# Weight chunks of the first expert layer: both words of the fp32 split kept in DRAM and loaded again, instead of one fp32 word that is split anew

## The chip, the cores and the metric

The kernel runs on one core of a Trainium2 chip. The metric is the device time of one execution in microseconds (us); lower is better. The core has five engines with a queue of instructions each: TensorE (PE: matmuls, and PEld, its weight loads), VectorE (DVE), ScalarE (ACT), GpSimd (POOL) and SyncE (SP), which here only issues DMAs. An engine takes its instructions in the order of its queue; semaphores tie the queues together.

## The reference, cut to what matters

```
x = attention(q, k, v)                                  # 4 x 8 heads, 576 tokens, keys and values pooled by 8
x: 2304 tokens x 512
x = (sigmoid(x @ w_gate) * (x @ w_val)) @ w_out         # "first layer": 512 -> 1536 -> 512
P = 8 rounds of row and column normalisation of exp(x @ gate)
out = sum over 8 experts of P[:, e] * (relu(x @ w1[e]) @ w2[e])
```

The three matrices of the first layer come in as float64. Every matmul of the layers is done on two fp32r words of each operand, the high word `hi` (the operand rounded) and the low word `lo` (the operand less `hi`), in three passes: hi.hi, hi.lo, lo.hi.

## The kernel before

The 2304 tokens are six blocks of 384. For each block j the first layer runs over twelve slices f of the hidden width. A pair (j, f) is a step, and there are 72. A step takes three weight chunks of 128 x 512, named g (gate), v (value) and o (out): 12 matmuls with g into a bank `pg`, 12 with v into `pv`, then sigmoid on ACT, the product with `pv` on DVE (line 821), the split of the product into `h` (ACT line 822, DVE line 825), and, one step later, 12 matmuls with o into four banks `big` (`x2_step`, line 560). The attention of the next block is cut into stages that are laid between these matmuls: scores (line 351), maximum and subtraction (369, 370), one exponential for the block (ACT line 393), sums (DVE 397), division (407), turning (PE 422, copied by ACT 424), product with the values (437), split into `xs` (ACT 447, DVE 448). The order of everything is the order in which the program writes it. The function `slot` decides how much narrowing and attention work goes between two matmul groups, by a running estimate `until` of when PE and DVE will be done.

**Narrowing.** Each of the 36 chunks (12 slices, three kinds) is read once as float64 (`load_wide`, four buffers `wide`) and made into fp32 `made` (four buffers) by `narrow_tick`: one scaling on ACT (185) and five operations on DVE (165, 166, 169, 175, 179; for the first twelve chunks 179 is on POOL). The steps of blocks 0, 1 and 2 are interleaved by slice, two slices at a time: `steps1` runs (0,0) to (0,3), (1,2), (1,3), (1,0), (1,1), (2,0) to (2,3), (1,4), (1,5), (0,4) and so on, so that a chunk is narrowed when its slice first comes up. From slice 2 on, blocks 0 and 1 share the chunk's tiles. Then come blocks 3, 4 and 5, whole.

**Splitting.** `split_chunk` takes the chunks in the order of the steps. At a chunk's first use it splits `made` into `wa_hi` (ACT 231) and `wa_lo` (DVE 236) and stores `made` to the DRAM tile `narrow` by a DMA on ACT's queue (233). At each of the 150 later uses `load_chunk` has brought `narrow` into one of four tiles `stage` (a DMA on SP's queue, 209), and the chunk is split again: `wa_hi` on ACT, `wa_lo` on DVE or, in blocks 3 to 5, for two chunks of three on POOL. There are nine pairs of tiles `wa`. `drop` gives a pair back once its matmuls are written.

After the 72 steps come 96 steps of the second layer (lines 903 and 934), whose weights are prepared on POOL, ACT and DVE as they go; the first layer's chunks play no part there.

Of the kernel before, what the change touches and what calls it, by code (L numbers as in the profile page):

```python
# [9 lines left out]
F32 = mybir.dt.float32  # L10
F32R = mybir.dt.float32r
U32 = mybir.dt.uint32
AF = mybir.ActivationFunctionType
ALU = mybir.AluOpType
# [6 lines left out]
def attention_moe_moe_kernel(  # L21
# [31 lines left out]
    nc = tc.nc  # L53
# [5 lines left out]
    E, FF2, _ = moe2_w2.shape  # L59
# [21 lines left out]
    base = base_pool.__enter__()  # L81
    dram = ctx.enter_context(tc.tile_pool(name="dram", bufs=1, space=DRAM))
    ps = ctx.enter_context(tc.tile_pool(name="ps", bufs=1, space=PSUM))

    def bank(tag, bufs):
        return ps.tile([128, 512], F32, tag=tag, name=tag, bufs=bufs)
# [11 lines left out]
    def f32(ap):  # L98
        return ap.bitcast(F32)
# [15 lines left out]
    chunks = []  # L115
# [3 lines left out]
    n_moe1 = len(chunks)  # L119
    n_wide = 3 * NF1  # L120
    WSRC = {"g": moe_w_gate, "v": moe_w_val, "o": moe_w_out}
    narrow = [dram.tile([128, 512], F32, name=f"narrow{i}") for i in range(n_wide)]
    NST = 4
    NWIDE = 4
    NMADE = 4
    NWA = 9
    xd = [[dram.tile([128, FX], F32, name=f"xd{p}_{i}") for i in range(7)] for p in range(NPAIR)]
    wsplit = {}
    staged = {}
    n_wload = [0]  # L130
    n_load = [0]
    n_split = [0]
    pools = {}
    later = []
# [53 lines left out]
    made = {}  # L188
    n_used = [0]

    def source(i):


        kind, j, f = chunks[i]
        return 3 * f + "gvo".find(kind), firsts[f] == j

    def load_chunk():

        i = n_load[0]
        while i < n_moe1 and source(i)[1]:  # L200
            i += 1
        n_load[0] = i
        if i >= len(chunks) or i - n_split[0] >= NST:
            return False
        if source(i)[0] >= n_used[0]:
            return False
        n_load[0] += 1
        t = base.tile([128, 512], F32, tag="stage", name="stage", bufs=NST)
        nc.sync.dma_start(out=t, in_=narrow[source(i)[0]])
        staged[i] = t  # L210
        return True

    def split_chunk():

        i = n_split[0]
        if i >= len(chunks):
            return False
        m, first = source(i)
        if first:
            if m not in made or (loaded and n_tick[0] == made[m][1]):  # L220
                return False
        elif i not in staged:
            return False
        if in_use[0] >= NWA:
            return False
        in_use[0] += 1
        n_split[0] += 1
        raw = made.pop(m)[0] if first else staged.pop(i)
        hi = base.tile([128, 512], F32R, tag="wa_hi", name="wa_hi", bufs=NWA)
        lo = base.tile([128, 512], F32R, tag="wa_lo", name="wa_lo", bufs=NWA)  # L230
        nc.scalar.activation(out=hi, in_=raw, func=AF.Copy)  # L231
        if first:
            nc.scalar.dma_start(out=narrow[m], in_=raw)
            n_used[0] += 1
        eng = nc.gpsimd if j > 2 and i % 3 else nc.vector
        eng.tensor_tensor(out=lo, in0=raw, in1=f32(hi), op=ALU.subtract)  # L236
        until["dve"] += 700
        wsplit[chunks[i]] = (hi, lo)
        return True

    in_use = [0]

    def stream(n):

        while load_chunk():
            pass
        for _ in range(n):
            if not split_chunk():
                return

# [418 lines left out]
    def load_w1(n):  # L669
        if n < len(steps2):  # L670
            _, e, q = steps2[n]
            raw1[n] = pools["late"].tile([128, 4, 2, 128], F32, tag="raw1", name="raw1", bufs=2)
            nc.sync.dma_start(out=raw1[n].rearrange("p a k f -> p (a k f)"), in_=moe2_w1[e, q])
# [9 lines left out]
    def prep_w1(n):  # L683


        if n >= len(steps2):
            return
        raw = raw1.pop(n)
        pool = pools["more" if n % 2 else "late"]
        a11, a12, a22, a21 = (raw[:, i] for i in range(4))  # L690
        ss = pools["late"].tile([128, 4, 2, 128], F32, tag="ss", name="ss", bufs=1)
        s1, s2, s4, s3 = (ss[:, i] for i in range(4))
        pl = nc.gpsimd.tensor_tensor
        fa = pool.tile([128, 2, 3, 2, 128], F32R, tag="fa", name="fa", bufs=1)
        fs = pool.tile([128, 2, 4, 2, 128], F32R, tag="fs", name="fs", bufs=1)
        wsum[n] = fa, fs
        nc.scalar.activation(out=fa[:, 0], in_=raw[:, 0:3], func=AF.Copy)
        pl(out=s1, in0=a21, in1=a22, op=ALU.add)
        pl(out=s3, in0=a11, in1=a21, op=ALU.subtract)
        yield  # L700
        pl(out=s2, in0=s1, in1=a11, op=ALU.subtract)
        pl(out=s4, in0=a12, in1=s2, op=ALU.subtract)
        yield
        nc.scalar.activation(out=fs[:, 0], in_=ss, func=AF.Copy)  # L704
        pl(out=fa[:, 1], in0=raw[:, 0:3], in1=f32(fa[:, 0]), op=ALU.subtract)  # L705
        yield
        pl(out=fs[:, 1, 0:2], in0=ss[:, 0:2], in1=f32(fs[:, 0, 0:2]), op=ALU.subtract)  # L707
        pl(out=fs[:, 1, 2:4], in0=ss[:, 2:4], in1=f32(fs[:, 0, 2:4]), op=ALU.subtract)  # L708
        yield
# [12 lines left out]
    def load_xf(p, i):  # L722
        if p < NPAIR:
            xf[p, i] = pools["late"].tile([128, 2, 2, TB], F32R, tag=f"xf{i}", name=f"xf{i}", bufs=1)
            nc.sync.dma_start(out=f32(xf[p, i]).rearrange("p s k c -> p (s k c)"), in_=xd[p][i])

    with tc.manual_schedule():
# [50 lines left out]
        for n, (j, f) in enumerate(steps1):  # L778
            now[0] = n
            if (j, f) == (NBLK - 1, 0):  # L780
                assert next(stages, "end") == "end"
                at_pool.__exit__(None, None, None)
                pools["late"] = ctx.enter_context(tc.tile_pool(name="late", bufs=1, reuse_waits="tile"))
                load_w1(0)
                load_w1(1)
                first_w = prep_w1(0)
            if j == NBLK - 1 and 2 <= f < 9:
                load_xf(0, (0, 3, 4, 2, 6, 1, 5)[f - 2])
            if j == NBLK - 1 and f >= NF1 - 4:
                next(first_w, None)  # L790
            if n_ready[0] <= j:
                while n_ready[0] <= j:
                    stage()
                n_stage[0] = 0
                until["pe"] = max(until["pe"], until["dve"])
            upto = 3 if n <= at_step[0, NF1 - 1] else max(4, j + 2)
            pg = bank("gv", 2)
            pv = bank("gv", 2)
            g = base.tile([128, TB], F32, tag="g", name="g", bufs=2)
            hi, lo = h_tiles()  # L800
            for key, pt in (("g", pg), ("v", pv)):
                while (key, j, f) not in wsplit:
                    if not split_chunk() and not load_chunk():
                        narrow_tick()
                    until["pe"] = max(until["pe"], until["dve"])
                w = wsplit[key, j, f]
                mm(
                    pt[:, :TB],
                    [
                        (tuple(t[:, kk * 128 : (kk + 1) * 128] for t in w[:2]), tuple(t[:, kk] for t in xs1[j]))  # L810
                        for kk in range(KT)
                    ],
                )
                drop((key, j, f))
                until["pe"] += 2080
                if key == "g":
                    nc.scalar.activation(out=g, in_=pg[:, :TB], func=AF.Sigmoid)
                else:
                    slot(1, upto)
                    until["dve"] = max(until["dve"], until["pe"]) + 1100  # L820
                    nc.vector.tensor_tensor(out=g, in0=g, in1=pv[:, :TB], op=ALU.mult)  # L821
                    nc.scalar.activation(out=hi, in_=g, func=AF.Copy)
                    while later:
                        later.pop(0)()
                    nc.vector.tensor_sub(out=lo, in0=g, in1=f32(hi))
                if key == "g":
                    slot(0, upto)
            if prev is not None:
                until["pe"] += 2080
                x2_step(*prev)  # L830
                if prev[1] == NF1 - 1:
                    gate = chain(gate, after_block(prev[0], prev[0] in (1, 3, 5)))
            gs[j, f] = (hi, lo)
            prev = (j, f)
            next(gate, None)
            slot(2, upto)
            stream(3)
# [280 lines left out]
```

## Time and profile before

| what | us |
|---|---|
| three timed runs | 2180.27, 2180.58, 2184.1 (median 2180.58) |
| the profiled execution, span | 2185.2 |
| PE busy in the span | 2096.2 |
| DVE busy | 1422.6 |
| ACT busy | 882.5 |
| POOL busy | 891.5 |

Busy PE is not PE at its best rate, since matmuls overlap; what PE loses shows as idle time before an instruction, with the instruction that released it, and as stretches at the lower of TensorE's two clocks. Start and end of a stretch are counted from the span's start. The first matmul of step 0 comes near 50 us, the steps of blocks 0 to 2 reach to about 345 us, blocks 3 to 5 to about 660 us, and the second layer fills the rest.

### The profile page before, as it was taken

What the parts mean: (1) busy time and instruction counts of PE and PEld (TensorE: products, weight loads), DVE (VectorE), ACT (ScalarE), POOL (GpSimd) and SP (SyncE); (2) the same over time, 40 slices, a digit from 0 to 9 for tenths busy, and PEclk for the clock granted to TensorE, in tenths of its full rate; (3) what the DMA queues carried; (4) which work ended last, traced back from release to release, by engine and by line L of the source; (5) the groups of instructions that cost most, each with busy time, mean ns of one, the idle gap of its engine ahead of it and who ended that gap; (6) DMA issues with size and microseconds to landing.
All of it is one profiled execution on the core that took longest, in us unless ns stands there. A gap on an engine that the chain in (4) does not pass through costs nothing.

```text
span 2185.2 us, 28656 instructions
## 1 busy us (share of the span) xinstructions
PE 2096.2 (96%) x10973; PEld 1905.0 (87%) x10973; DVE 1422.6 (65%) x2172; ACT 882.5 (40%) x1607; POOL 891.5 (41%) x780
## 2 busy tenths in 40 slices
PE   4679999999999999999999999999999999999999
PEld 4568989988997888888888898989888888898988
DVE  6846876644435877666666666666666666666665
ACT  4334343454544444434343434343433343434342
POOL 1100000353554465454545454545454545454541
PEclk8679999999999999999999999999999999999999
DMA  7432553453562132121215121212125212121211
GB/s 227 143 119 85 167 171 116 131 181 106 194 228 92 59 116 78 61 75 60 76 59 206 58 78 58 78 58 78 58 78 188 77 58 78 58 78 58 78 58 39
DMA packets 87451, 222.09 MB, mean 102 GB/s; under 512 B 8849, under 2 KB 8849, under 8 KB 87313
## 3 DMA queue, kind: packets, MB, share of 16 engines
q1 hardware_dynamic: 82128, 210.81, 28.5%
q10 hardware_dynamic: 5184, 9.44, 1.2%
q8 instruction: 86, 1.41, 0.3%
q14 instruction: 53, 0.43, 0.1%
HBM read 189.55 MB, written 30.67 MB: 101 GB/s over the span
## 4 chain that ended last, share of the span: by engine, by line
PE 86%; DVE 6%; issue 3%; ACT 2%; DMA 1%; POOL 1%; SPq 0%; ACTq 0%; DVEq 0%; POOLq 0%
PE big L934 37%; PE at L903 18%; PE gv L903 14%; PE gv L268 10%; PE big L560 4%; DVE wa_lo L236 1%; PE at L351 1%; DMA narrow<-made 1%; PE at L437 1%; DVE made L166 1%; DVE made L165 1%; DVE g L821 1%; ACT wa_hi L231 1%; PE at L422 0%; DVE wide L175 0%
## 5 line engine op out<-in xcount | busy, mean ns | idle before, releaser
L934 PE MATMUL big<-w2hl,h 128*128 128x512 f32 x3456 | 893.8, 394 | 0.0
L934 PEld LDWEIGHTS big<-w2hl,h 128*128 128x128 f32 x3456 | 642.0, 188 | 102.2
L963 DVE SCALAR_TENSOR_TENSOR acc<-big,prob,acc 128x512 f32<-128x512 f32 x516 | 385.6, 748 | 264.8 <-PE big L934 258.7
L705 POOL TENSOR_TENSOR fa<-raw,fa 128x768 fp32r<-128x768 f32 x96 | 179.4, 1869 | 440.0 <-PE big L934 403.2
L268 PE MATMUL gv<-xs,wa_hi 128*128 128x384 f32 x1152 | 314.6, 355 | 20.9 <-ACT xs L447 8.1
L707 POOL TENSOR_TENSOR fs<-ss,fs 128x512 fp32r<-128x512 f32 x96 | 125.0, 1303 | 292.9 <-ACT fs L704 289.3
L268 PEld LDWEIGHTS gv<-xs,wa_hi 128*128 128x128 f32 x1152 | 217.1, 198 | 28.2 <-ACT xs L447 8.9
L917 ACT ACTIVATE h<-gv 128x384 fp32r<-128x384 f32 x192 | 94.3, 491 | 355.2 <-DVE gv L1045 196.4
L903 PE MATMUL at<-xf,fa 128*128 128x384 f32 x1152 | 233.7, 338 | 0.8 <-DVE c L1038 0.8
L903 PE MATMUL at<-xf,fs 128*128 128x384 f32 x1152 | 232.4, 337 | 0.4 <-ACT c L1011 0.4
L903 PE MATMUL gv<-xf,fs 128*128 128x384 f32 x1152 | 231.6, 336 | 0.0
L717 DVE TENSOR_TENSOR w2hl<-raw,w2hl 128x512 fp32r<-128x512 f32 x192 | 227.6, 1186 | 6.1 <-ACT w2hl L716 6.1
L903 PEld LDWEIGHTS at<-xf,fa 128*128 128x128 f32 x1152 | 206.6, 189 | 17.7 <-DVE c L1038 1.6
L903 PEld LDWEIGHTS gv<-xf,fs 128*128 128x128 f32 x1152 | 205.4, 188 | 16.3
L268 PE MATMUL gv<-xs,wa_lo 128*128 128x384 f32 x576 | 203.1, 353 | 14.8 <-DVE wa_lo L236 11.8
L903 PEld LDWEIGHTS at<-xf,fs 128*128 128x128 f32 x1152 | 204.4, 188 | 9.0 <-ACT c L1011 0.7
L918 DVE SCALAR_TENSOR_TENSOR h<-gv,h 128x384 fp32r<-128x384 f32 x192 | 107.2, 558 | 107.6 <-ACT h L917 107.6
L560 PE MATMUL big<-h,wa_hi 128*128 128x384 f32 x576 | 150.8, 343 | 0.0
L594 POOL TENSOR_TENSOR fx<-x,fx 128x768 fp32r<-128x768 f32 x10 | 18.4, 1844 | 316.5 <-DVE x L577 263.4
L236 POOL TENSOR_TENSOR wa_lo<-stage,wa_hi 128x512 fp32r<-128x512 f32 x67 | 99.6, 1499 | 81.3 <-ACT wa_hi L231 69.6
L268 PEld LDWEIGHTS gv<-xs,wa_lo 128*128 128x128 f32 x576 | 114.7, 199 | 17.7 <-DVE wa_lo L236 14.6
L708 POOL TENSOR_TENSOR fs<-ss,fs 128x512 fp32r<-128x512 f32 x96 | 125.5, 1307 | 0.0
(149 smaller groups left out, 2682.1 us busy)
## 6 DMA issues: line engine op xcount, KB each, us to landing
raw<-in_moe_w_dram SPq DMA_DIRECT2D x192, 512.0 KB, 3.8
stage<-narrow SPq DMA_DIRECT2D x150, 256.0 KB, 2.8
xd<-fx SPq DMA_DIRECT2D x21, 768.0 KB, 3.3
xf<-xd SPq DMA_DIRECT2D x21, 768.0 KB, 6.6
narrow<-made ACTq DMA_DIRECT2D x36, 256.0 KB, 2.0
wide<-in_moe_w_gate_dram SPq DMA_DIRECT2D x12, 512.0 KB, 3.8
wide<-in_moe_w_val_dram SPq DMA_DIRECT2D x12, 512.0 KB, 10.0
wide<-in_moe_w_out_dram SPq DMA_DIRECT2D x12, 512.0 KB
```

The lines of the kernel that those rows point to most:

```text
L236: eng.tensor_tensor(out=lo, in0=raw, in1=f32(hi), op=ALU.subtract)
L268: nc.tensor.matmul(out=out_, lhsT=a[s], rhs=b[m], start=(i == 0), stop=(i == n - 1))
L560: nc.tensor.matmul(out=x2p[d][:, :TB], lhsT=w[s][:, d * 128 : (d + 1) * 128], rhs=gs[j, f][m], start=(first and i == 0), stop=(last and i ...
L705: pl(out=fa[:, 1], in0=raw[:, 0:3], in1=f32(fa[:, 0]), op=ALU.subtract)
L707: pl(out=fs[:, 1, 0:2], in0=ss[:, 0:2], in1=f32(fs[:, 0, 0:2]), op=ALU.subtract)
L708: pl(out=fs[:, 1, 2:4], in0=ss[:, 2:4], in1=f32(fs[:, 0, 2:4]), op=ALU.subtract)
L717: nc.vector.tensor_sub(out=t[:, 1, i], in0=raw[:, i], in1=f32(t[:, 0, i]))
L903: nc.tensor.matmul(out=pt[:, :TB], lhsT=w[:, s, i, k], rhs=t[:, o, k], start=(start and m == 0), stop=(m == 5), skip_group_check=True,)
L917: nc.scalar.activation(out=t[:, 0], in_=src, func=AF.Relu)
L918: nc.vector.scalar_tensor_tensor(out=t[:, 1], in0=src, scalar=0.0, in1=f32(t[:, 0]), op0=ALU.max, op1=ALU.subtract)
L934: nc.tensor.matmul(out=py, lhsT=h[:, s, cs], rhs=w2hl[n][:, o, fh], start=(m == 0), stop=(m == 5))
L963: nc.vector.scalar_tensor_tensor(out=acc[t], in0=py, scalar=pr, in1=acc[t], op0=ALU.mult, op1=ALU.add)
```

## The change

At a chunk's first use it is split as before (ACT, then always DVE), into one tile `wa` of two words, and the store of both words together (512 KB instead of 256 KB) goes to a DRAM tile `words`, on SP's queue instead of ACT's, two chunks later (`keep(1)`; a load that needs a word that is not stored yet first writes all stores that are pending). At each of the 150 later uses one DMA of 512 KB on SP's queue fills the `wa` tile; the tile `stage`, the split on ACT and the subtraction on DVE or POOL are gone. The tiles `wa` become eleven in place of nine; four `stage` tiles go. `stream(n)` now counts first uses only, and loads are written as far ahead as tiles are free. A load no longer adds 700 to the estimate `until["dve"]`.

```diff
-    narrow = [dram.tile([128, 512], F32, name=f"narrow{i}") for i in range(n_wide)]
-    NST = 4
+    words = [dram.tile([128, 1024], F32, name=f"words{i}") for i in range(n_wide)]
-    NWA = 9
+    NWA = 11
...
-    def load_chunk():
...
-        t = base.tile([128, 512], F32, tag="stage", name="stage", bufs=NST)
-        nc.sync.dma_start(out=t, in_=narrow[source(i)[0]])
-        staged[i] = t
-        return True
+    stores = []
+    n_kept = [0]
+
+    def keep(k):
+
+        while len(stores) > k:
+            m, w = stores.pop(0)
+            nc.sync.dma_start(out=words[m], in_=f32(w).rearrange("p s c -> p (s c)"))
+            n_kept[0] += 1
...
-        elif i not in staged:
+        elif m >= n_used[0]:
             return False
         if in_use[0] >= NWA:
             return False
         in_use[0] += 1
         n_split[0] += 1
-        raw = made.pop(m)[0] if first else staged.pop(i)
-        hi = base.tile([128, 512], F32R, tag="wa_hi", name="wa_hi", bufs=NWA)
-        lo = base.tile([128, 512], F32R, tag="wa_lo", name="wa_lo", bufs=NWA)
-        nc.scalar.activation(out=hi, in_=raw, func=AF.Copy)
-        if first:
-            nc.scalar.dma_start(out=narrow[m], in_=raw)
-            n_used[0] += 1
-        eng = nc.gpsimd if j > 2 and i % 3 else nc.vector
-        eng.tensor_tensor(out=lo, in0=raw, in1=f32(hi), op=ALU.subtract)
+        w = base.tile([128, 2, 512], F32R, tag="wa", name="wa", bufs=NWA)
+        wsplit[chunks[i]] = (w[:, 0], w[:, 1])
+        if not first:
+            keep(0 if m >= n_kept[0] else len(stores))
+            nc.sync.dma_start(out=f32(w).rearrange("p s c -> p (s c)"), in_=words[m])
+            return True
+        raw = made.pop(m)[0]
+        nc.scalar.activation(out=w[:, 0], in_=raw, func=AF.Copy)
+        n_used[0] += 1
+        nc.vector.tensor_tensor(out=w[:, 1], in0=raw, in1=f32(w[:, 0]), op=ALU.subtract)
         until["dve"] += 700
-        wsplit[chunks[i]] = (hi, lo)
+        keep(1)
+        stores.append((m, w))
         return True
...
     def stream(n):
 
-        while load_chunk():
-            pass
-        for _ in range(n):
+        k = n_used[0] + n
+        while n_used[0] < k:
             if not split_chunk():
                 return
```

The order of PE's instructions is the same before and after. What changes stands on the other queues. Line numbers of the changed kernel are 3 to 8 lower than those of before (393 becomes 385, 397 becomes 389, 817 becomes 809, 821 becomes 813).

DVE before, at steps (1,3) and (1,0), where the exponentials of block 2 (`e`) are summed and divided:

```order
L236 TENSOR_TENSOR wa_lo<-stage,wa_hi 128x512 x2
L821 TENSOR_TENSOR g<-g,gv 128x384
L825 TENSOR_TENSOR h_1053<-g,h_1052 128x384
L236 TENSOR_TENSOR wa_lo<-stage,wa_hi 128x512 x2
L397 TENSOR_REDUCE den<-e 128x8 x3
```

DVE of the changed kernel, at the same place:

```order
L362 TENSOR_TENSOR e<-at,mx 128x288
L813 TENSOR_TENSOR g<-g,gv 128x384
L817 TENSOR_TENSOR h_1015<-g,h_1014 128x384
L389 TENSOR_REDUCE den<-e 128x8 x3
L394 TENSOR_SCALAR den<-den 128x24
```

The four subtractions for loaded chunks are gone from ahead of the product and of the sums.

ACT before, at the exponential of block 4:

```order
L393 ACT_TABLE_LOAD
L393 ACTIVATE e<-e 128x1728
L593 ACTIVATE fx<-tt 128x768
L231 ACTIVATE wa_hi<-stage 128x512 x3
L817 ACT_TABLE_LOAD
L817 ACTIVATE g<-gv 128x384
```

ACT of the changed kernel, at the same place:

```order
L385 ACT_TABLE_LOAD
L385 ACTIVATE e<-e 128x1728
L585 ACTIVATE fx<-tt 128x768
L809 ACT_TABLE_LOAD
L809 ACTIVATE g<-gv 128x384
```

Three splits of loaded chunks no longer stand between the exponential and the next sigmoid.

SP before, in the second half of the narrowing (`wide` loads of float64 chunks, `stage` loads, `qt` a query tile):

```order
L147 DMA wide<-in_moe_w_out_dram 128x1024
L147 DMA wide<-in_moe_w_gate_dram 128x1024
L311 DMA qt<-in_q_dram 128x512
L147 DMA wide<-in_moe_w_val_dram 128x1024
L209 DMA stage<-narrow_89 128x512
```

SP of the changed kernel, at the same place:

```order
L144 DMA wide<-in_moe_w_out_dram 128x1024
L201 DMA words_96<-wa 128x1024
L144 DMA wide<-in_moe_w_gate_dram 128x1024
L201 DMA words_97<-wa 128x1024
L303 DMA qt<-in_q_dram 128x512
L144 DMA wide<-in_moe_w_val_dram 128x1024
L201 DMA words_98<-wa 128x1024
```

A store of 512 KB stands behind each `wide` load on the same queue, where the store of 256 KB was on ACT's.

## Rows read from the trace of the kernel before

**Rows 1.** The page: the span.
```profile
span 2185.2 us, 28656 instructions
```

**Rows 2.** Stretches: busy us (instructions) by engine, granted clock, DMA share, GB/s.
```profile
75.00:185.00 110.00, 81.68 (x452) 72.41 (x453) 58.23 (x104) 40.04 (x65) 4.39 (x3) 0.78 0.38 122
185.00:345.00 160.00, 150.19 (x841) 144.93 (x840) 129.45 (x235) 62.19 (x118) 0.00 (x0) 0.98 0.43 140
345.00:660.00 315.00, 309.90 (x1913) 293.96 (x1912) 152.32 (x227) 143.37 (x257) 142.48 (x96) 0.99 0.47 163
```

**Rows 3.** The chain that ended last: start, us, what.
```profile
238.40 2.08 PE big L560 x12
```

**Rows 4.** Waits of PE, 75 to 660 us: in total, times, longest.
```profile
PE at L422 <- DVE e L407: 17.9, 4, 8.1
PE gv L268 <- DVE g L821: 6.6, 5, 2.3
...
PE at L437 <- ACT a L424: 3.6, 6, 1.2
...
PE gv L268 <- ACT g L817: 1.1, 1, 1.1
```

**Rows 5.** Stretches, instructions on `stage` alone: DVE, ACT, POOL busy us (instructions), then as above.
```profile
75.00:185.00 110.00, 9.23 (x14) 8.60 (x14) 0.00 (x0) 0.78 0.38 122
185.00:345.00 160.00, 11.57 (x19) 10.78 (x19) 0.00 (x0) 0.98 0.43 140
345.00:660.00 315.00, 51.06 (x53) 68.06 (x118) 99.56 (x67) 0.99 0.47 163
```

**Rows 6.** Instructions of PE in order of time: start, us, what [idle before <- releaser].
```profile
126.04 2.00 PE L351 MATMUL at<-kp,qt 64*128 64x72 f32 x16
...
132.57 2.48 PE L351 MATMUL at<-kp,qt 64*128 64x72 f32 x16 [1.18 <-DVE e L370]
...
159.04 1.04 PE L422 MATMUL at<-ident,e 128*72 128x128 f32 x4 [8.07 <-DVE e L407]
...
447.23 0.60 PE L422 MATMUL at<-ident,e 128*72 128x128 f32 x4 [2.75 <-DVE e L407]
```

**Rows 7.** Instructions of DVE in order of time.
```profile
130.88 0.69 DVE L236 TENSOR_TENSOR wa_lo<-stage,wa_hi 128x512 fp32r<-128x512 f32 x1 [2.08 <-ACT wa_hi L231]
...
154.88 0.69 DVE L236 TENSOR_TENSOR wa_lo<-stage,wa_hi 128x512 fp32r<-128x512 f32 x1 [1.63 <-ACT wa_hi L231]
155.49 2.06 DVE L397 TENSOR_REDUCE den<-e 128x8 f32<-128x576 f32 x3
...
320.40 0.43 DVE L165 TENSOR_SCALAR made<-wide 128x512 uint32<-128x512 uint32 x1 [3.48 <-DMA narrow<-made]
...
443.47 2.06 DVE L397 TENSOR_REDUCE den<-e 128x8 f32<-128x576 f32 x3
```

**Rows 8.** Instructions of ACT in order of time.
```profile
150.36 1.65 ACT L393 ACTIVATE e<-e 128x1728 f32<-128x1728 f32 x1
...
438.68 1.65 ACT L393 ACTIVATE e<-e 128x1728 f32<-128x1728 f32 x1
```

**Rows 9.** Two short stretches, columns as in rows 2.
```profile
130.00:145.00 15.00, 13.82 (x62) 12.76 (x61) 6.01 (x13) 3.26 (x7) 0.00 (x0) 0.66 0.21 69
...
447.00:453.00 6.00, 5.77 (x28) 5.74 (x29) 5.41 (x7) 3.04 (x6) 3.63 (x2) 0.72 0.29 93
```

**Rows 10.** DMA issues, whole span: KB each, median us from issue to landing.
```profile
raw<-in_moe_w_dram SPq DMA_DIRECT2D x192, 512.0 KB, 3.8
stage<-narrow SPq DMA_DIRECT2D x150, 256.0 KB, 2.8
```

**Rows 11.** Waits of ACT, 75 to 345 us.
```profile
ACT wide L185 <- DMA wide<-in_moe_w_val_dram: 13.1, 3, 7.2
```

**Rows 12.** The stretch in which block 5 runs beside the second layer's first loads.
```profile
597.00:641.00 44.00, 44.00 (x256) 42.70 (x255) 13.61 (x21) 19.98 (x36) 22.66 (x17) 1.00 0.81 290
```

**Rows 13.** DMA issues in that stretch.
```profile
stage<-narrow SPq DMA_DIRECT2D x21, 256.0 KB, 3.6
```

More of the change, by code (lines that the diff above doesn't have):

```diff
@@ L121, in attention_moe_moe_kernel @@
     WSRC = {"g": moe_w_gate, "v": moe_w_val, "o": moe_w_out}
-    narrow = [dram.tile([128, 512], F32, name=f"narrow{i}") for i in range(n_wide)]
-    NST = 4
+    words = [dram.tile([128, 1024], F32, name=f"words{i}") for i in range(n_wide)]
     NWIDE = 4
     NMADE = 4
-    NWA = 9
+    NWA = 11
     xd = [[dram.tile([128, FX], F32, name=f"xd{p}_{i}") for i in range(7)] for p in range(NPAIR)]
     wsplit = {}
-    staged = {}
     n_wload = [0]
-    n_load = [0]
     n_split = [0]
@@ L195, in source @@
         return 3 * f + "gvo".find(kind), firsts[f] == j
-    def load_chunk():
[L199 to L207, printed above, removed]
-        t = base.tile([128, 512], F32, tag="stage", name="stage", bufs=NST)
-        nc.sync.dma_start(out=t, in_=narrow[source(i)[0]])
-        staged[i] = t
-        return True
+    stores = []
[5 more added lines that the diff above has]
+            n_kept[0] += 1
     def split_chunk():
@@ L802, in attention_moe_moe_kernel @@
                 while (key, j, f) not in wsplit:
-                    if not split_chunk() and not load_chunk():
+                    if not split_chunk():
                         narrow_tick()
```

## The prediction

> **What bounds the kernel now.** I read the stretches first. From 345 us on PE is busy for 309.9 of 315 us, at full clock but for a hundredth; between 185 and 345 us for 150.2 of 160; between 75 and 185 us for only 81.7 of 110, and there at 0.78 of the clock [rows 2]. The chain of work that ended last runs over PE nearly throughout once the first blocks are done, so nothing that is taken off another engine after 345 us is worth its own busy time. It is worth what PE waits for it. The reader is to see two kinds of loss in the list of PE's waits: PE waits for a result of DVE or ACT [rows 4], and after such a gap it runs for some us at the lower clock [rows 9]. The change removes work from DVE, ACT and POOL, so the question is at which of PE's waits that work stood in the queue ahead of the instruction that PE waited for.
>
> **What is removed, and what it hides behind.** For each of the 150 loads [rows 10] it is a split on ACT and a subtraction on DVE or POOL. They take 87 us of ACT, 72 of DVE and 100 of POOL, summed over the three stretches [rows 5]. Most of it lies under matmuls: between 345 and 660 us 118 chunks are split [rows 5], and PE's idle time there is about 5 us [rows 2]. So these 259 us of busy time are no gain by themselves. POOL's share I cost at nothing: no wait of PE in the list is for POOL after its first chunks. If POOL's cover were gone nothing would change, since the other work that it does there is needed a step or more later.
>
> **The waits, one by one.**
>
> *Scores of block 2.* At 132.57 PE waits 1.18 us for the subtraction L370. The scores that this subtraction reads were finished at 128.04, the end of the pair of score groups that began at 126.04 [rows 6]. On DVE a subtraction of a loaded chunk stood ahead, idle until 130.88 for ACT's split [rows 7], which in turn needed a tile that PE was still reading. All of that goes: 1.2 us. The 15 us around it show a granted clock of 0.66, that is, two thirds of the time at 1.2 GHz instead of 2.4 [rows 9]. A stretch of length T at mean clock c loses (1 - c) T, here 5.1 us. The fall begins about where the gap is; whether it would have come without it cannot be read, so the bounds are 0 and 5.1, and I take six tenths, 3.1.
>
> *Turning of block 2.* At 159.04 PE waits 8.07 us for the division [rows 6]. The chain behind it: the exponential ends on ACT at 150.36 + 1.65 = 152.01 [rows 8], but the sums begin on DVE only at 155.49, behind a subtraction at 154.88 that waited for a split queued on ACT behind the exponential, the table load and a sigmoid [rows 7]. In the new order the sums come next after the product, so they start at the exponential's end: 155.49 - 152.01 = 3.5 us. The rest of the gap stays.
>
> *Copies on ACT.* PE waits 3.6 us in six for the copies L424 [rows 4]. In two or three of the six a split of a loaded chunk (8.60 us for 14, 0.61 each [rows 5]) stands directly ahead on ACT. Bounds 0 and 3.6; I take two splits, 1.2.
>
> *Sigmoid after the exponential of block 3.* One wait of 1.1 us for L817 [rows 4]; ACT has two splits of loaded chunks between the exponential and the table load, as in block 4's order shown above. Gone: 1.1.
>
> *The product L821.* 6.6 us in five waits [rows 4], all between 185 and 345 us, where DVE is busy for 129.45 of 160 us [rows 2]. There the change takes 19 subtractions, 11.6 us [rows 5], and one wait of 3.48 us for the buffer `made`, which the store of the narrow word held back [rows 7]; in the new kernel `made` is free as soon as it is split. DVE's queue gets 15 us shorter while its narrowing work is the same. Against a full recovery stands that the new order puts two narrowings (some 3.5 us each) into one step at two places. Bounds 0 and 6.6; I take two thirds, 4.4.
>
> *Turning of block 4.* At 447.23 PE waits 2.75 us [rows 6]. The exponential ends at 438.68 + 1.65 = 440.33 [rows 8], the sums begin at 443.47 [rows 7], 3.1 us later, behind a subtraction that waited for the three splits in the order above. The sums move up by more than the gap: 2.75 us gone. The next 6 us run at 0.72 of the clock [rows 9]: (1 - 0.72) x 6 = 1.7 us, which go with the gap that made them. Together 4.5.
>
> The sum is 1.2 + 3.1 + 3.5 + 1.2 + 1.1 + 4.4 + 4.5 = 19.0 us.
>
> **What is added and moved.** The narrowing of a chunk at first use keeps its operations. One subtraction moves from POOL to DVE near the start, about 0.6 us on DVE where it is busy anyway. The store moves from ACT's queue to SP's; SP's own work is waiting. The order on PE is unchanged, and so are its matmuls. New is that PE waits for a DMA instead of DVE, ACT or POOL. With eleven tiles a load is written once a chunk is given back; the tightest one comes at the end of a step for a chunk that is used after seven groups of 12 matmuls, at 2.08 us a group [rows 3] 14.6 us later. A 512 KB load lands after 3.8 us [rows 10], so 10.8 us are spare. SP takes its queue in order, so behind a load that waits for PE stand the `wide` loads, the query tiles and the stores `xd`; before, they stood in the same way behind `stage` loads. For all this I set -2 us, with bounds 0 and 5.
>
> The net gain is 17.0 us. The sum is made against the profiled execution, 2185.2 us [rows 1], whose span is 4.6 above the median of the three timed runs; I take the difference as it is to that median: 2180.6 - 17.0 = **2163.6 us**.
>
> **Rivals.**
>
> *Slower: the stores hold up the float64 loads.* Before, a store of 256 KB went on ACT's queue beside a `wide` load on SP's; now 512 KB go on SP's own queue. 256 KB more take 1.0 us more to land (3.8 against 2.8 [rows 10]), so a whole store ahead of a `wide` load costs it 2.0 us. ACT, which scales the chunk, stops for it with sigmoids and copies queued behind: it waited 13.1 us in three such waits already [rows 11]. If all 24 chunks that are narrowed after the first twelve came 2.0 us later on the path, 48 us would be lost and the time were 2180.6 - 17 + 48 = 2212; from nine chunks on, the gain is gone. Against it: in the new order each store stands behind the load of its own turn, and the next load comes a narrowing later, more than the 2.0 us that the store takes. The Trainium skill (DMA: Bandwidth & Descriptors, Queues, rings and completion order) says that a DMA engine takes turns between the queues of the issuing engines, packet by packet, but works off one queue in order; by that rule the store is no longer shared out but wholly ahead, which is this rival's mechanism, and no row here shows two transfers of one queue overtaking or not. Chance 10%.
>
> *Loads late in block 5.* There the DMA engines are busy for 0.81 of 44 us and move 290 GB/s, 12.8 MB [rows 12]; at that mix they would move 290 / 0.81 = 358 GB/s when always busy. 21 loads [rows 13] grow by 0.262 MB each, to 18.3 MB: 51.1 us at 358 GB/s, 7.1 late by the end, less than the 10.8 spare, so nothing. If the rate stayed at 290, they would be 19 late and PE would stall for 8.3: 2171.9. Chance 13%.
>
> *It moves little.* The gaps on PE fill with the next thing that is late, as DVE's narrowing comes earlier and the clock falls elsewhere. For it speaks that between 75 and 185 us attention's own chain (exponential, sums, division, turning) leaves gaps that no split caused; against it, that three of the terms are read off the queue directly. Gain 0 to 4: 2178.6. Chance 13%.
>
> **Chances and range.** My forecast has 64%. Its own range is from the terms' bounds: only what stands directly in the queue, 1.2 + 3.5 + 1.1 + 2.75 = 8.6, less 0 to 2, up to all terms in full, 1.2 + 5.1 + 3.5 + 3.6 + 1.1 + 6.6 + 4.5 = 25.6: 2155 to 2174. With the second and part of the third rival above it, and 3 us below for clock that comes back elsewhere, 2152 to 2179 holds eight in ten. A difference of 0.2%, 4.4 us, is about what a measurement of this kernel can tell from none. Faster by more: 64 + 13 and a part of the third rival, 0.78; within: 0.12; slower: 0.10.
>
> **What would show it.** Right: PE's wait for L407 falls from 17.9 to about 11, with the sums starting at the exponential's end in blocks 2 and 4; its wait for L821 falls below 3; no L370 wait near 132 us; clock near 1.00 after the turning of block 4; blocks 3 to 5 without new waits. Wrong: PE waiting for loads of `wa`, ACT waiting longer for `wide` than before, or the 75 to 185 us stretch unchanged in length while DVE and ACT are emptier in it.

## The result and the profile after

The changed kernel takes 2157.39 us (median of four, 2154.92 to 2157.66) against 2180.69 (median of four) beside it: ratio 0.9894, 95% interval 0.9879 to 0.9909, so 23.3 us faster; forecast were 17.0.

Page of the changed kernel, then its stretches (busy us (instructions) of PE, PEld, DVE, ACT, POOL, granted clock, DMA share, GB/s), which answer to [rows 1, 2].

```profile
span 2155.7 us, 28264 instructions
```

```profile
75.00:185.00 110.00, 87.70 (x522) 78.77 (x521) 55.99 (x101) 38.55 (x64) 4.37 (x3) 0.86 0.60 190
185.00:345.00 160.00, 155.56 (x897) 151.83 (x898) 117.51 (x215) 53.33 (x97) 3.67 (x2) 0.98 0.67 219
345.00:660.00 315.00, 308.80 (x1903) 290.57 (x1901) 105.52 (x184) 87.85 (x154) 49.22 (x35) 1.00 0.73 260
```

PE is busier in the first two stretches by 6.0 and 5.4 us, so more of the program fits into them; in the third it was full before and still is, though DVE loses 47 us there, ACT 56 and POOL 93. Waits of PE from 75 to 660 us, the answer to [rows 4]:

```profile
PE at L414 <- DVE e L399: 9.9, 2, 6.3
PE gv L260 <- DVE g L813: 5.8, 3, 3.7
...
PE at L429 <- ACT a L416: 2.8, 6, 0.9
```

The wait for the division fell from 17.9 to 9.9. The wait for the product, which I had put at below 3, is 5.8, and one of its three pieces is longer than any before. Instructions of PE, DVE and ACT of the changed kernel in order of time, which answer to [rows 6 to 8]:

```profile
147.35 0.87 PE L414 MATMUL at<-ident,e 128*72 128x128 f32 x4 [3.61 <-DVE e L399]
...
186.62 3.89 PE L260 MATMUL gv<-xs,wa 128*128 128x384 f32 x11 [3.69 <-DVE g L813]
...
279.38 2.37 PE L260 MATMUL gv<-xs,wa 128*128 128x384 f32 x12 [1.20 <-DVE g L813]
...
306.50 2.35 PE L260 MATMUL gv<-xs,wa 128*128 128x384 f32 x12 [0.95 <-DVE g L813]
...
422.96 0.60 PE L414 MATMUL at<-ident,e 128*72 128x128 f32 x4
```

```profile
143.79 2.07 DVE L389 TENSOR_REDUCE den<-e 128x8 f32<-128x576 f32 x3 [2.40 <-ACT e L385]
...
179.57 0.69 DVE L228 TENSOR_TENSOR wa<-made,wa 128x512 fp32r<-128x512 f32 x1 [5.24 <-ACT wa L226]
...
186.02 0.55 DVE L813 TENSOR_TENSOR g<-g,gv 128x384 f32<-128x384 f32 x1
...
419.02 2.07 DVE L389 TENSOR_REDUCE den<-e 128x8 f32<-128x576 f32 x3 [2.41 <-ACT e L385]
```

```profile
142.11 1.65 ACT L385 ACTIVATE e<-e 128x1728 f32<-128x1728 f32 x1
...
178.91 0.63 ACT L226 ACTIVATE wa<-made 128x512 fp32r<-128x512 f32 x1 [3.66 <-DMA words<-wa]
179.45 0.47 ACT L809 ACTIVATE g<-gv 128x384 f32<-128x384 f32 x1
```

In blocks 2 and 4 the sums start as the exponential ends (142.11 + 1.65 = 143.76, sums at 143.79); the gap at the turning of block 2 is 3.61 instead of 8.07, the one of block 4 (2.75) is gone. New is the gap of 3.69. Some eight us before it ACT wanted to split a fresh chunk into a tile and waited 3.66 us for a *store* out of that tile. SyncE's rows (the `q` marks its DMA queue) and its waits from 150 to 175 us show why the store was late:

```profile
161.34 11.54 SPq L223 DMA_DIRECT2D wa<-words  x5
172.97 0.86 SPq L201 DMA_DIRECT2D words<-wa  x2
```

```profile
SPq L223 <- PE gv L260: 20.8, 5, 7.5
```

Two stores stand in SP's queue behind loads that wait for PE to give tiles back. Sigmoid and narrowing queue up behind ACT's split: DVE waits 5.24 us for it, then has narrowing operations of two chunks and three low words ahead of the product, and PE gets the product late.

### The profile page after: what moved, and what is told of

Its sections match the earlier page's. It is cut to its first block, busy times and chain, and to the rows that moved or that the text cites. A ratio compares the mean times of both kernels' runs of the same rounds, so it can differ in the third digit from the quotient of the medians.

```text
span 2155.7 us, 28264 instructions
## 1 busy us (share of the span) xinstructions
PE 2083.4 (97%) x10973; PEld 1895.9 (88%) x10973; DVE 1349.1 (63%) x2090; ACT 802.9 (37%) x1457; POOL 791.0 (37%) x712
## 4 chain that ended last, share of the span: by engine, by line
PE 91%; DVE 3%; issue 2%; DMA 2%; ACT 1%; POOL 0%; SPq 0%; DVEq 0%; ACTq 0%; POOLq 0%
PE big L926 37%; PE at L895 19%; PE gv L895 14%; PE gv L260 12%; PE big L552 6%; PE at L343 1%; PE at L429 1%; DMA wide<-in_moe_w_gate_dram 1%; PE at L414 1%; DMA wide<-in_moe_w_val_dram 0%; PE at L260 0%; DVE wa L228 0%; DVE made L163 0%; DVE wide L172 0%; DMA words<-wa 0%
## 5 line engine op out<-in xcount | busy, mean ns | idle before, releaser
L260 PE MATMUL gv<-xs,wa 128*128 128x384 f32 x1728 | 339.0, 350 | 29.8 <-DVE wa L228 8.9
L260 PEld LDWEIGHTS gv<-xs,wa 128*128 128x128 f32 x1728 | 311.9, 196 | 37.7 <-DVE wa L228 11.1
L895 PEld LDWEIGHTS gv<-xf,fs 128*128 128x128 f32 x1152 | 205.4, 188 | 16.3
L552 PE MATMUL big<-h,wa 128*128 128x384 f32 x864 | 168.0, 344 | 0.0
L552 PEld LDWEIGHTS big<-h,wa 128*128 128x128 f32 x864 | 155.2, 194 | 1.1 <-issue 0.3
L813 DVE TENSOR_TENSOR g<-g,gv 128x384 f32<-128x384 f32 x72 | 39.7, 551 | 151.9 <-PE gv L260 151.9
L708 ACT ACTIVATE w2hl<-raw 128x512 fp32r<-128x512 f32 x192 | 120.7, 629 | 0.0
```

The lines of the kernel that those rows point to most:

```text
L260: nc.tensor.matmul(out=out_, lhsT=a[s], rhs=b[m], start=(i == 0), stop=(i == n - 1))
L552: nc.tensor.matmul(out=x2p[d][:, :TB], lhsT=w[s][:, d * 128 : (d + 1) * 128], rhs=gs[j, f][m], start=(first and i == 0), stop=(last and i ...
L708: nc.scalar.activation(out=t[:, 0, i], in_=raw[:, i], func=AF.Copy)
L895: nc.tensor.matmul(out=pt[:, :TB], lhsT=w[:, s, i, k], rhs=t[:, o, k], start=(start and m == 0), stop=(m == 5), skip_group_check=True,)
```

## The experiments

**The measure.** For each trace I took the time between the same five instructions of PE: a, the first matmul of block 1's first step (122.05 before); b, the first turning of block 2 [rows 6]; c, the turning of block 3 at 349.11; d, the first matmul of block 4's first step (487.21); e, the first gate matmul after block 5 (671.32). Line numbers in a row are those of its own kernel.

| kernel | 0 to a | a to b | b to c | c to d | d to e | timed median |
|---|---|---|---|---|---|---|
| before, first trace | 122.05 | 36.99 | 190.07 | 138.10 | 184.11 | 2180.69 |
| before, second trace (e9) | 123.22 | 35.34 | 186.93 | 138.12 | 182.57 | 2181.43 (one run) |
| after | 118.84 | 28.51 | 180.41 | 133.61 | 181.78 | 2157.39 |
| e4 estimate as before | 120.78 | 28.64 | 181.77 | 133.59 | 181.78 | 2160.16 |
| e3 nine tiles | 118.22 | 25.44 | 186.50 | 133.61 | 181.79 | 2165.08 |
| e5 eleven tiles, store on POOL | 120.51 | 25.45 | 172.10 | 133.61 | 184.86 | 2152.25 |
| e6 the same on ACT | 119.88 | 25.46 | 174.36 | 133.61 | 181.77 | 2153.95 |
| e13 the same on SP | 124.53 | 26.60 | 179.12 | 133.61 | 181.75 | 2162.27 |
| e10 nine tiles, store on POOL | 124.63 | 26.73 | 178.12 | 133.61 | 181.78 | 2157.86 |
| e11 e10 and the busy time | 127.08 | 26.77 | 187.25 | 134.08 | 181.79 | 2174.15 |
| e12 e10 and half more loads | 120.28 | 25.43 | 178.29 | 133.61 | 191.67 | 2166.61 |
| e1 ready in 0 to 2, two stores | 120.95 | 28.52 | 199.15 | 140.16 | 182.57 | 2184.88 |
| e7 ready in 0 to 2, one store | 118.42 | 28.54 | 187.29 | 142.44 | 182.56 | 2174.05 |
| e8 ready in 3 to 5 | 122.23 | 35.63 | 187.53 | 133.61 | 181.79 | 2178.10 |

### The kernel before, a second time (e9)

> The kernel before, unchanged, for a second trace of it: its timed executions lie between 2175.6 and 2185.6, and the one on which the prediction stands was 2185 with its overhead. Theory (PE's gaps are set by the order of the queues and come back within 0.3 us each; what differs from one execution to the next is where the clock falls, and a few us of the 29.5 between the two profiled spans are that): 8.07, 2.75 and the waits for L821 come back, the half-clock stretches of 1.5 us or more move. Rival (the gaps themselves are chance): the sum of PE's gaps up to 700 us, 83.9, moves by 5 or more.

Its span is 2179.6, 5.6 below the first. Waits of PE, 75 to 660 us, as in [rows 4]:

```profile
PE at L422 <- DVE e L407: 17.8, 4, 8.1
PE gv L268 <- DVE g L821: 7.2, 5, 2.8
```

Behind a the gaps come back (8.07 and 2.75 to the hundredth, two others 0.5 and 0.6 longer); before a they do not all, where five differ by 0.8 to 2.0 us, both ways. All of PE's gaps up to 700 us sum to 83.2, 83.9 before. What moved is the clock: (1 - c) T for the granted clock c, over 75 to 700 us, is 29.0 against 32.4. So the theory holds behind a but for those two, and the difference of the two profiled spans, 29.5, has 5.6 us in it that are not the change's. Against this second trace the change saves 23.9: 4.4 up to a, 6.8, 6.5, 4.5 and 0.8 in the stages, 0.9 behind e. That this is near the timed 23.3 says less than it seems: "0 to a" runs from 118 to 127 over all kernels in no order that I can name (e10 and e12 do the same work there but for some added loads and differ by 4.3), and is no evidence. What the stages show as the change's is the gain from a to d, 17.9 against this trace and 22.6 against the first.

### Where the store stands (e5, e6, e13)

```diff
-            nc.sync.dma_start(out=words[m], ...)
+            nc.gpsimd.dma_start(out=words[m], ...)   # e6: nc.scalar; e13: nc.sync as before
...
-        keep(1)
         stores.append((m, w))
+        keep(0)
```

> The changed kernel, with the store of the two words written directly behind the split, on POOL's queue, in place of one or two chunks later on SP's. In the changed kernel's trace ACT waits 3.7 us near 179 for a store of `words` to end before it may split into the stored tile, sigmoid and narrowing queue up behind it, and PE then waits 3.69 us for the product L813 and runs 4.8 us at the lower clock (2.2 lost). Theory (the change's own new wait: stores stand on SP's queue behind loads that wait for PE): the gap at 186.62 and the lower clock behind it go, 4 to 6 us faster than the changed kernel, about 2152. Rival (two narrowings in one slot make the gap, whatever the store does): the gap stays at 3 us or more and the time within 2 us of the changed kernel.

> The same with the store on ACT's queue, where the old store was. Theory: the tile is free as early, but the issue waits on ACT's queue for DVE's subtraction (1 to 5 us behind the split), and sigmoids and copies wait behind it: between the changed kernel and 10 us slower, 2157 to 2167. Rival (only SP's queue matters): as fast as with POOL's queue, within 2 us.

> Eleven tiles, the store directly behind the split as in the runs with POOL's and ACT's queue, but on SP's. In the changed kernel two stores stand on SP behind ten loads of `wa` that wait for PE to give tiles back; written at once, they stand ahead of these. Theory (what costs is that those stores come late, not whose queue they are on): the gap of 3.69 us before the product goes, within 2.5 us of POOL's queue, 2150 to 2155. Rival (on SP's queue a store in any place delays float64 loads or is delayed by loads): 2156 or more, with the gap still there or ACT waiting longer for `wide`.

POOL's queue: 2152.25, ratio 0.9870 (0.9852 to 0.9889), 5.1 below the changed kernel, as the theory had it. PE's wait for the product, all told, is 0.5 us, and ACT no longer waits for a store; b to c is 8.3 shorter. Against that stand 3.1 us more from d to e, where this trace has a granted clock of 0.98 and the changed kernel 1.00. ACT's queue: 2153.95, ratio 0.9880 (0.9862 to 0.9898); here the rival was right and my theory wrong: ACT does wait for DVE before it issues, but has time for it. Waits of ACT in that kernel, 75 to 345 us:

```profile
ACT g L809 <- DVE wa L228: 12.7, 5, 3.9
```

SP's queue, at once: 2162.27, ratio 0.9916 (0.9895 to 0.9938), slower than the changed kernel (all six runs lie above its four). The rival is right: it is not only that stores come late. Waits of SP and of ACT in e13, 75 to 345 us, then ACT in e13, ACT in the changed kernel at the same place, and PE's gap in e13:

```profile
SPq L201 <- DVE wa L228: 121.3, 29, 12.2
```

```profile
ACT wide L182 <- DMA wide<-in_moe_w_val_dram: 18.2, 3, 8.9
```

```profile
300.31 0.68 ACT L182 ACTIVATE wide<-wide 128x512 f32<-128x512 f32 x1 [4.26 <-DMA wide<-in_moe_w_val_dram]
```

```profile
300.47 0.70 ACT L182 ACTIVATE wide<-wide 128x512 f32<-128x512 f32 x1 [0.57 <-DMA wide<-in_moe_w_val_dram]
```

```profile
306.32 1.97 PE L260 MATMUL gv<-xs,wa 128*128 128x384 f32 x5 [4.62 <-DVE g L813]
```

SP stands for 121 us at stores whose words DVE has not made, and the float64 loads behind them come late (ACT waits 18.2 us for them; 11.2 in the changed kernel). One of these waits, 4.26 us at 300.31, holds up the next split and low word, and with them the product that PE waits 4.62 us for; b to c is 7.0 longer than in e5. Against the changed kernel the trace does not place the loss: from a to e it is 3.2 shorter, and 5.7 longer up to a. On SP a store is either late itself or makes others late; of the three queues tried it is the worst for one. e5 is the fastest kernel of the study, beside e6, which its interval does not tell apart.

### Tiles and estimate (e3, e10, e4)

```diff
-    NWA = 11
+    NWA = 9                      # e3; e10 with the store of e5
...
             nc.sync.dma_start(out=f32(w)..., in_=words[m])
+            until["dve"] += 700  # e4, eleven tiles
             return True
```

> The changed kernel with nine tiles `wa` in place of eleven. Theory: the two tiles only give loads more time; a load then comes some two groups of 12 matmuls later, 14.6 - 4.2 = 10.4 us ahead of its use at the tightest, and lands in about 4: within 2 us of the changed kernel. Rival (the two tiles are the gain, since chunks are there earlier): 5 us or more slower than the changed kernel, and PE waits for a load of `wa`.

> Store at once on POOL's queue, with nine tiles in place of eleven. Theory (with nine tiles a tile that was just stored comes round sooner, so the late store on SP's queue cost 7.7 us more with nine tiles; look-ahead itself is worth nothing): within 2.5 us of the eleven tiles with the same store, 2150 to 2155. Rival (the look-ahead of the loads is what eleven tiles bring): 5 us or more slower, 2157 to 2162.

> The changed kernel, where each load adds 700 again to the estimate of DVE's end, as each split did before, so that narrowing and attention are laid between the matmuls as if the subtractions were still there. Theory: the gain stays but for 0 to 4 us, and two narrowings in one place (the new gap of 3.69 us at 186.62) come apart again, so it may even be 2 to 4 us faster. Rival (the gain is the earlier narrowing that the lower estimate allows): 8 us or more of the gain is lost.

Nine tiles: 2165.08, ratio 0.9929 (0.9901 to 0.9957), 7.7 slower than the changed kernel, and its trace loses 6.1 from b to c. That is the rival's size, but PE waits for no load of `wa`; so neither account was right. With the store on POOL nine tiles take 2157.86, ratio 0.9897 (0.9871 to 0.9923), 5.6 more than eleven: again the rival's side. DVE in e10, then in e5, at the same step: from the narrowing's first operation (L162) to the chunk's low word (L228) and on to the product that PE waits for (L813).

```profile
208.61 0.42 DVE L162 TENSOR_SCALAR made<-wide 128x512 uint32<-128x512 uint32 x1
...
212.18 0.43 DVE L162 TENSOR_SCALAR made<-wide 128x512 uint32<-128x512 uint32 x1
...
215.04 0.68 DVE L228 TENSOR_TENSOR wa<-made,wa 128x512 fp32r<-128x512 f32 x1
...
216.51 0.54 DVE L813 TENSOR_TENSOR g<-g,gv 128x384 f32<-128x384 f32 x1
```

```profile
203.56 0.41 DVE L162 TENSOR_SCALAR made<-wide 128x512 uint32<-128x512 uint32 x1
...
206.41 0.68 DVE L228 TENSOR_TENSOR wa<-made,wa 128x512 fp32r<-128x512 f32 x1
...
207.87 0.54 DVE L813 TENSOR_TENSOR g<-g,gv 128x384 f32<-128x384 f32 x1
```

With nine tiles two narrowings stand ahead of one product, with eleven one. `split_chunk` writes nothing while all tiles are in use, so fewer tiles put a chunk's work into a later place of the program. In e10 PE waits 1.07 us at 194.23, 0.89 at 217.10, 0.84 at 280.54 and 1.52 at 308.21 for the product (before: 1.38, 0.89, 1.67 and 2.30 in four of its five); in e5 none of these is above 0.3. At this step, then, the tiles work through the order on DVE. From b to c the tiles are worth 6.1 us (e3 against the changed kernel) and 6.0 (e10 against e5), the store off SP 8.4 (e3 against e10) and 8.3 (the changed kernel against e5): either is worth the same with or without the other.

The estimate: 2160.16, ratio 0.9899 (0.9879 to 0.9919), 2.8 slower by the medians and 1.1 by the ratios, which the intervals do not tell from none, within the theory's 0 to 4; its second half (narrowings come apart) is refuted, since a gap of 4.29 stands at the same place.

### Half of the change (e1, e7, e8)

```diff
         if not first and j in READY:      # e1, e7: blocks 0 to 2; e8: 3 to 5 (words stored in block 2, POOL's queue)
             nc.sync.dma_start(out=f32(w)..., in_=words[m])
             return "load"
+        raw = made.pop(m)[0] if first else staged.pop(i)
+        # the split on ACT and on DVE or POOL as before; e7: from the high word, a product for the subtraction
```

> Ready-made words are loaded in blocks 0 to 2 alone; in blocks 3 to 5 the fp32 word is loaded and split anew as before the change, with nine tiles and four stage tiles, and both stores are made (so `made` is held by its store as before). Theory (the gain comes from splits that stood in the queues of DVE and ACT ahead of what PE waited for, most of it in the steps of blocks 0 to 2): 14 to 18 of the 23 us are kept, about 2165; the turning of block 2 gains its 8 to 9 us, the turning of block 4 keeps its gap of 2.75. Rival (tiles and look-ahead, or relief of POOL in blocks 3 to 5): under 8 us kept, 2173 or more.

> Ready-made words in blocks 0 to 2 alone, this time without the second store that held `made` in the first such run: in blocks 3 to 5 only the stored high word is loaded (256 KB, four stage tiles) and goes through ACT and DVE or POOL with the operations and durations of before. The low word there is a product of the high word in place of the true low word, so the output is off in these blocks; nine tiles. Theory (most of the gain is earned in blocks 0 to 2): 14 to 18 us faster than before, about 2164, with the 2.75 us gap at the turning of block 4 back. Rival (ready-made words in blocks 0 to 2 bring nothing by themselves, as the first such run reads): within 4 us of before.

> The other half: blocks 0 to 2 load and split the fp32 word as before; at the uses in block 2 the two words are stored once (POOL's queue), and blocks 3 to 5 load them ready-made; nine tiles and four stage tiles. Theory: the 8 us gap at the turning of block 2 stays, the 2.75 us gap at the turning of block 4 goes: 4.5 to 7 us faster than before, about 2174. Rival (the busy time taken off DVE, ACT and POOL is what counts, and 219 of its 259 us lie here): 15 us or more.

e1 gains nothing: 2184.88, ratio 1.0021 (1.0008 to 1.0033). Its first stage is as short as the changed kernel's, 28.52, but b to c is 9 to 12 longer than before: ACT waits 11.3 us there for stores of `words`, DVE 8.0 for the second store to give `made` back, and PE 18.2 for the product, 6.69 of it at 191.53. The new wait of the change, made larger, eats the gain.

e7, without the second store: 2174.05, ratio 0.9973 (0.9961 to 0.9986), 6 us faster, not 14 to 18. a to b gains its 7 to 8; b to c gains nothing, as in e3 with the same nine tiles and SP's stores; and a new gap of 4.12 at 372.45 comes from mixing, since the first stage loads stand on SP behind ready-made loads that wait for tiles (ACT waits 9.2 us for one).

e8: 2178.10, ratio 0.9997 (0.9986 to 1.0009). c to d is 133.61, to the hundredth that of the changed kernel, and a to b as before. The timing, though, is against the theory's 4.5 to 7 us: its interval ends at 3.1 us faster. The profiled execution, 2176.31, is the fastest of twelve; whether the added stores in blocks 0 to 2 take the rest stays open. So the 4.5 us are shown by the stage, not by the time of the whole. A first form of this half (e2, both stores made at first use) deadlocks and has no time.

### The busy time put back (e11)

```diff
             nc.sync.dma_start(out=f32(w)..., in_=words[m])
+            nc.scalar.activation(out=sink_a, in_=src, func=AF.Copy)
+            eng, sink = (nc.gpsimd, sink_p) if j > 2 and i % 3 else (nc.vector, sink_d)
+            eng.tensor_tensor(out=sink, in0=src, in1=src, op=ALU.subtract)
             return True
```

> As the run with nine tiles and POOL's store, and for each of the 150 loads a copy of 128x512 on ACT and a subtraction of 128x512 on DVE (in blocks 3 to 5 two of three on POOL) between scratch tiles: the busy time that the change removed is back, but it waits for nothing and nothing waits for it. Theory (half of the gain or more is waits that such a split dragged into the queue, for a tile that PE still read and for ACT; the rest is the bare time ahead of what PE waits for, above all where DVE is busy for 118 of 160 us): 4 to 10 us slower than without the dummies, 2157 to 2162. Rival (busy time alone explains the change): 18 us or more slower, 2170 or more. Rival (it is only the waits): within 2 us.

2174.15, ratio 0.9964 (0.9950 to 0.9979): 16.3 slower than e10, outside the theory's 4 to 10 and below the rival's 18; its profiled span, one of its shorter ones, is 12.5 longer. The stages sort it. From b to c the bare time costs 9.1 us; from a to b nothing, from c to d 0.5, from d to e nothing, though most of the 150 dummies lie behind c (118 chunks were split there before [rows 5]). The stretches b to c of e10 and of e11:

```profile
151.36:329.48 178.12, 170.58 (x1012) 163.92 (x1012) 126.08 (x228) 61.42 (x114) 12.79 (x24) 0.99 0.65 221
```

```profile
153.85:341.10 187.25, 174.65 (x1013) 166.96 (x1013) 141.65 (x252) 74.50 (x138) 12.79 (x24) 0.97 0.62 210
```

Where DVE is busy for 126 of 178 us, 15.6 us more on it and 13.1 on ACT cost 9.1, of which (1 - c) T puts 3.8 on the clock (0.97 against 0.99); where it is busy for 50 of 134 (c to d), 24.6 us more cost 0.5. And at the turnings of blocks 2 and 4 the waits do not return (10.0 us in two for the division, as without dummies): there it was what the split waited for, not its length.

### Half as many bytes again (e12)

```diff
             nc.sync.dma_start(out=f32(w)..., in_=words[m])
+            spare = base.tile([128, 512], F32, tag="spare", name="spare", bufs=4)
+            nc.sync.dma_start(out=spare, in_=words[m][:, 0:512])
```

> As the run with nine tiles and POOL's store, and each of the 150 loads is followed on SP's queue by a second load of its first 256 KB into a scratch tile that nobody reads: half as many bytes again. Theory (the doubled loads are hidden with room to spare): from 345 to 660 us 118 loads x 0.262 MB / 315 us = 98 GB/s more, 358 in all, which is just the rate worked out for always busy DMA engines; late loads begin to show in block 5, 0 to 10 us slower. Rival (the loads as they are stand at the limit already): 20 us or more slower, with PE waiting for `wa` loads all through blocks 3 to 5.

2166.61, ratio 0.9935 (0.9914 to 0.9956), 8.8 slower than e10, in the theory's range. Waits of PE and the stretch of blocks 3 to 5:

```profile
PE gv L262 <- DMA wa<-words: 7.3, 4, 3.6
```

```profile
345.00:660.00 315.00, 301.51 (x1842) 284.35 (x1841) 100.47 (x176) 83.42 (x145) 47.33 (x34) 0.99 0.93 348
```

The four waits come at 602.29, 617.78, 625.64 and 633.29, in block 5 and nowhere else. The change's own loads are hidden, and there is room for less than half as many bytes again.

## Why the prediction was right, step by step

The direction and the mechanism held: waits that removed splits had dragged into DVE's and ACT's queues. 17.0 was forecast, 23.3 came, inside the range and inside the forecast's own range. The stretches that the terms are about, a to d, gained 17.9 against the second trace and 22.6 against the first; that 17.0 comes so near is luck in part, as the paragraph on the product shows.

*Scores and turning of block 2* (1.2 + 3.1 + 3.5 = 7.8): a to b is 6.8 shorter than in the second trace, 8.5 than in the first. The scores' wait for the subtraction, 1.18, is gone; 0.58 for other scores stands there instead. The turning's gap shrank by 4.5: the sums' 3.5, and the exponential now ends with PE's last matmul instead of 1.0 after it. The clock term is the weak one. The stretch of [rows 9] had a clock of 0.66; in the second trace of before the same 15 us had 0.77 with the same gap; in the changed kernel 127 to 142 us has 0.89, and in e5, with PE as busy (14.42 of 15 us), 1.00. One trace's clock was taken for the gap's doing.

*Turning of block 4* (2.75 + 1.7): c to d fell from 138.1 to 133.6, by 4.5, in every kernel with ready-made words in blocks 3 to 5 and no dummies, and in e8, which has them there alone. Its size was right, and the same in both traces of before.

*Copies, sigmoid, product* (1.2 + 1.1 + 4.4, less 2): 4.7 expected, 6.5 by the second trace, 9.7 by the first. The total is of that size; the parts are not. The sigmoid's wait is gone and the copies' fell by 0.8. Of before's five product waits, four (at 205.64, 213.62, 228.53 and 308.99) are gone and the fifth fell from 2.30 to 0.95: 5.7 us, more than the 4.4. But two new ones came, 3.69 and 1.20, so that the wait only went from 6.6 (7.2 in e9) to 5.8; both are gone in e5. I had argued that a queue shorter by 15 us gives the wait back. e3 and e7 show that with nine tiles b to c gains nothing, and e10 that it gains 9 as soon as the stores leave SP; e11 that they go again when the bare busy time is put back. So the shorter queue does give it back, and two things that I had not priced decide whether PE gets it: the store that a reused tile waits for (8 us from b to c) and the two tiles (6 us). They pull opposite ways, and that is the luck in the sum. I had looked at the tiles only as time for loads.

*What was added* (2, bounds 0 to 5) is the mis-sized term: 5.1 by e5's time, at the bound, 8.3 from b to c, and by another way than those I named. I let loads, float64 loads and query tiles wait on SP, but not a split for the store out of its tile.

*The slower rival* is not in the change, where ACT's wait for the `val` chunks is 11.2 us, 13.1 before; e13 builds it by writing the store early, and then that wait is 18.2. By the Trainium skill (DMA: Bandwidth & Descriptors, Queues, rings and completion order) each DMA engine takes the descriptors of a queue in order. What e13 shows is held up one step earlier, at SP's issue, which waits for DVE, and no run here tells how two started transfers share an engine.

*Loads late in block 5*: not so, and the rate in that rival's sums was too low (last section). *It moves little*: refuted by the timing. Of the signs, four came (division 9.9 where about 11 was said, no wait of the scores for the subtraction, clock 1.00 after block 4's turning, no new waits in blocks 3 to 5); the product below 3 did not.

## What to carry to other kernels

Work taken off an engine that is not the bound is worth the waits that it dragged into the queue; its bare time counted here only in the stage where that engine was the busier, 9 us where DVE was busy for 126 of 178 us and 0.5 where for 50 of 134. A store out of a tile that comes round again is a wait of the next writer: put it directly behind its data, on a queue that holds no loads others wait for. And before a gap's clock is priced, look at a second trace of the same kernel: from block 1 on the gaps came back to 0.6 us, the places where the clock falls did not.

## What the runs showed of the hardware

The estimate of 358 GB/s for always busy DMA engines, from 290 GB/s at a share of 0.81 [rows 12], was too low. Block 5 of the changed kernel, 40 us (columns as in [rows 2]):

```profile
571.00:611.00 40.00, 40.00 (x233) 38.70 (x232) 7.40 (x14) 8.30 (x16) 8.34 (x7) 1.00 1.02 413
```

The DMA engines are full for 40 us and PE does not lose a tenth of one: 413 GB/s with 512 KB and 768 KB transfers. The Trainium skill (Perfetto Trace Analysis, Roofline) gives 358 GB/s as a core's share when both cores of a pair draw on the memory, and about 435 as the bound of its 16 DMA engines when one core is alone. The trace, of a kernel on one core, agrees with the second: 413 is above the one and below the other. Granted clock: with the same 14.42 us of PE work in 15, it was 0.89 in one kernel and 1.00 in another, so PE's idle time in a stretch did not settle at which of the two levels, 1.2 or 2.4 GHz, it ran there.
